# Two row halves of the systolic array taken out of step: one does first products while the other does second products

## The chip, the cores and the metric

The kernel runs on one core of a Trainium2 chip. The metric is the device time of one execution in microseconds (us); lower is better. Three timed executions of the kernel before took 2473.54, 2473.85 and 2474.29 us, median 2473.85 us.

## The reference, cut to what matters

Four sequences of 4096 rows with 192 channels go through a causal convolution over seven positions, with softmax weights by head, and then through two MLPs without bias, 192 to 2048 to 192. Everything is float32.

```python
out = np.einsum('hk,bskhg->bshg', w, x_unf)      # seven taps, 8 heads
x = out.reshape(B * S, D)                        # 16384 x 192
h = x @ w_in1;  x = (h * np.cos(h)) @ w_out1     # first MLP
h = x @ w_in2                                    # second MLP, ELU
out = np.where(h > 0.0, h, np.exp(np.minimum(h, 0.0)) - 1.0) @ w_out2
```

The weights of both MLPs arrive as 64-bit floats (two 32-bit words each) and are decoded on the core.

## The kernel before, in words

**Tiles.** The 16384 tokens are cut into 32 blocks of 512. A block's 192 channels lie on the partitions, as 128 own ones ("o") and 64 more. Every float32 operand is split into a rounded part and a rest (names ending in h and l: xh and xl, gh and gl, wi "h" and "l"), and a product is made of two or three products of parts. All these matmuls contract over 64 rows, so two of them lie side by side on the two row halves of the array (`half`, partitions 0 to 63 and 64 to 127), each with 512 columns of tokens, each into a PSUM bank of its own.

**Steps.** The 2048 hidden columns of an MLP are cut into 16 tiles of 128. A step (m, b, j) is MLP m, block b, and the two hidden tiles 2j and 2j+1. There are 2 x 32 x 8 = 512 steps. The first products of step s (`emit_A`, line 497) are nine matmuls for each of the two tiles: three for the own channels "o", three for the 64 more "c", three for the other half's channels "s" (their copies sh and sl are made by a DMA that swaps the halves). Both tiles advance together, one on each row half, into the banks u and v. The second products of step s - 2 (`emit_B`, line 553; LAG is 2) follow: ten matmuls for each row half, for both tiles, into four accumulators: a0 and a1 belong to row half 0, b0 and b1 to row half 1; a0 and b0 sum the first 128 output channels, a1 and b1 the last 64.

**Between the two products.** A tile u goes through ScalarE and VectorE. First MLP: `emit_act1` (ScalarE, rounds), `emit_mid` (VectorE, subtracts), `emit_act2` (ScalarE, Sin), `emit_g` (VectorE, multiplies with u). Second MLP: `emit_act1` (Relu of -u), `emit_act2` (Exp), `emit_g` (VectorE, the ELU). Then `emit_hi` rounds to gh on ScalarE and `emit_lo` subtracts to gl on GpSimd. `emit_g` is the last reader of the bank. In step s the queues get the gh and gl of step s - 1, and then the two tiles of step s.

**Blocks and groups.** GROUP is 4: the steps run four blocks through the first MLP (a phase of 32 steps), then the same four through the second, eight groups in all. At the end of a block `evac` (line 567) copies a0 and a1 to SBUF on ScalarE and adds b0 and b1 to them on VectorE; `sums` (line 580) then adds the halves, makes zh, zl and zc for the second MLP, or transposes and writes the output. `chore` hands out such work, one piece at a time, between the steps' own instructions.

**Convolution.** The generator `convs` computes the blocks to come, one VectorE instruction (a tap) at a time, each call of `next(cq)` in the second MLP's phases giving one. The first four blocks are done at the start from rows that are transposed on TensorE: `conv_by_products` makes the taps as matmuls for c0, c1, a1, a2 and a3 ("a" is the first 128 channels, "c" the last 64); a0 and c2 go on VectorE.

**Weights.** `pieces` lists 26 pieces of the first MLP's weights and 24 of the second's. `advance` moves three pieces on by one stage each: it decodes one (`decode`, line 163: three or four VectorE instructions, one or two on ScalarE, one on GpSimd), and splits another into its h and l parts. In the first eight steps `advance` is called three times a step, later once, until `prepared`. `need` calls it until the pieces that a step reads are done. The second MLP's pieces start once blocks 0 to 3 are convolved.

**PSUM.** There are eight banks: four accumulators, two for u, one for v (`ps_h`), and one that serves the decoding (`ps_w`) and becomes a second one for v from step 8 on (`top.close()` in `step`; only every other step uses it).

**Order.** The program fixes the order itself (`tc.manual_schedule()`): every engine runs its instructions in the order in which the code names them, and TensorE's queue holds both row halves' matmuls in one order.

## Time and profile before

| | |
|---|---|
| median of three timed executions | 2473.85 us (2473.54 to 2474.29) |
| the profiled execution's own time | 2472.95 us |
| its span, first to last instruction | 2471.2 us |
| mean granted TensorE clock over the span | 0.987 of 2.4 GHz |
| TensorE, matmuls | busy 2349.8 us, 95% |
| VectorE (DVE) | busy 1696.9 us, 69% |
| ScalarE (ACT) | busy 1926.3 us, 78% |
| GpSimd (POOL) | busy 1587.4 us, 64% |

Records of matmuls overlap: one takes 0.39 us in the trace, and two run at a time, one on each row half. In the rows below PE is TensorE, PEld its weight loads, DVE VectorE, ACT ScalarE, POOL GpSimd; "a<-b" is output and input by the program's names, with buffer numbers left out (u, v: the banks of first products; a, b: accumulators of row half 0 and 1; w: a tile between the products; y<-xT,wch: a tap; e: an evacuated sum), and L565 is line 565.

### The profile page before, as it was taken

To read this page: it belongs to the slowest core of one execution; us is meant where nothing else is said; L and a number is where in the kernel's file an instruction comes from. 1 tells how busy PE (TensorE), PEld (TensorE's weight loads), DVE (VectorE), ACT (ScalarE), POOL (GpSimd) and SP (SyncE) were. 2 spreads that over 40 slices of the span, in tenths; PEclk is the share of its full clock that TensorE was granted. 3 is DMA by queue.
4 is the path that set the end of the run, shared out by engine and by line. 5 is a ranking of instruction groups with operands and counts; after the bars stand their busy time and mean duration, and the time that the engine had idled before them with its cause. 6 is when DMAs were issued, how large, how long until landed. Compare 5 with 4: busy or idle time off the path is not lost.

```text
span 2471.2 us, 51323 instructions
## 1 busy us (share of the span) xinstructions
PE 2349.8 (95%) x19614; PEld 1955.0 (79%) x19614; DVE 1696.9 (69%) x2324; ACT 1926.3 (78%) x3529; POOL 1587.4 (64%) x1271
## 2 busy tenths in 40 slices
PE   7888999999999999999999999999999999999998
PEld 4565678777798878987788777987789787888898
DVE  5688895767766586766866678666777668666433
ACT  5566768887788877888788787888778887888886
POOL 4567655666666666666666676666666666667665
PEclk8899999999999999999999999999999999999999
DMA  5012322111221131211221213121222112112011
GB/s 143 26 52 60 71 48 59 42 35 30 60 50 31 27 60 36 54 35 41 45 57 29 48 30 60 37 50 27 38 57 54 31 38 44 41 32 52 19 37 24
DMA packets 279494, 111.89 MB, mean 45 GB/s; under 512 B 231888, under 2 KB 246224, under 8 KB 279248
## 3 DMA queue, kind: packets, MB, share of 16 engines
q1 hardware_dynamic: 278928, 108.35, 20.4%
q8 instruction: 153, 2.51, 0.4%
q14 instruction: 93, 0.76, 0.1%
q10 hardware_dynamic: 320, 0.26, 0.0%
HBM read 29.91 MB, written 12.58 MB: 17 GB/s over the span
## 4 chain that ended last, share of the span: by engine, by line
PE 67%; DVE 12%; ACT 8%; issue 6%; POOL 5%; DMA 0%; SPq 0%; DVEq 0%; POOLq 0%; ACTq 0%
PE a L565 27%; PE u L506 24%; PE v L506 8%; PE b L565 8%; POOL gl L550 4%; ACT gh L545 2%; DVE y L360 2%; DVE e L576 2%; ACT e L584 2%; DVE w L539 2%; DVE w L523 1%; DVE w L185 1%; ACT e L573 1%; DVE w L537 1%; ACT w L516 1%
## 5 line engine op out<-in xcount | busy, mean ns | idle before, releaser
L550 POOL TENSOR_TENSOR gl<-w,gh 128x512 fp32r<-128x512 f32 x1024 | 1348.8, 1322 | 825.6 <-ACT gh L545 741.4
L545 ACT ACTIVATE gh<-w 128x512 fp32r<-128x512 f32 x1024 | 640.3, 625 | 173.6 <-DVE w L537 106.6
L565 PE MATMUL a<-gh,wo_hl 64*128 64x512 f32 x2048 | 638.7, 391 | 2.2 <-ACT gh L545 2.2
L565 PE MATMUL b<-gh,wo_hl 64*128 64x512 f32 x2048 | 636.4, 391 | 0.9 <-DVE e L576 0.9
L565 PE MATMUL a<-gl,wo_hl 64*128 64x512 f32 x1024 | 408.7, 399 | 46.5 <-POOL gl L550 45.2
L565 PEld LDWEIGHTS a<-gh,wo_hl 64*128 64x128 f32 x2048 | 374.3, 185 | 59.9 <-ACT gh L545 19.6
L565 PE MATMUL b<-gl,wo_hl 64*128 64x512 f32 x1024 | 407.7, 398 | 0.0
L506 PE MATMUL u<-sh,wi_o 64*128 64x512 f32 x1024 | 399.8, 390 | 3.7 <-DMA sh<-xh 3.7
L506 PE MATMUL v<-ch,wi_c 64*128 64x512 f32 x1024 | 400.7, 391 | 0.0
L506 PE MATMUL u<-ch,wi_c 64*128 64x512 f32 x1024 | 400.0, 391 | 0.0
L506 PE MATMUL v<-sh,wi_o 64*128 64x512 f32 x1024 | 399.7, 390 | 0.0
L565 PE MATMUL b<-gh,wo_s 64*128 64x512 f32 x1024 | 397.2, 388 | 0.0
L565 PE MATMUL a<-gh,wo_s 64*128 64x512 f32 x1024 | 396.9, 388 | 0.0
L565 PE MATMUL a<-gl,wo_s 64*128 64x512 f32 x1024 | 396.5, 387 | 0.0
L565 PE MATMUL b<-gl,wo_s 64*128 64x512 f32 x1024 | 395.9, 387 | 0.0
L565 PEld LDWEIGHTS b<-gh,wo_hl 64*128 64x128 f32 x2048 | 373.5, 185 | 18.8 <-DVE e L576 3.0
L360 DVE SCALAR_TENSOR_TENSOR y<-xT,wch,y 128x512 f32<-128x512 f32 x264 | 382.1, 1447 | 0.9
L523 DVE SCALAR_TENSOR_TENSOR w<-u,w 128x512 f32<-128x512 f32 x256 | 177.0, 691 | 248.8 <-ACT w L514 247.1
L531 ACT ACTIVATE w<-w 128x512 f32<-128x512 f32 x512 | 323.7, 632 | 16.1
L539 DVE SCALAR_TENSOR_TENSOR w<-w,u 128x512 f32<-128x512 f32 x256 | 174.5, 682 | 193.5 <-ACT w L531 190.5
L529 ACT ACTIVATE w<-w 128x512 f32<-128x512 f32 x512 | 294.7, 629 | 1.6 <-DVE w L523 1.5
L565 PEld LDWEIGHTS a<-gl,wo_hl 64*128 64x128 f32 x1024 | 189.0, 185 | 111.9 <-POOL gl L550 93.0
(129 smaller groups left out, 6930.0 us busy)
## 6 DMA issues: line engine op xcount, KB each, us to landing
out_dram<-e SPq DMA_DIRECT2D x192, 64.0 KB, 1.9
xa<-in_x_dram SPq DMA_DIRECT2D x112, 88.0 KB, 2.6
sh<-xh SPq DMA_DIRECT2D x64, 128.0 KB, 2.3
sl<-xl SPq DMA_DIRECT2D x64, 128.0 KB, 2.3
sh<-zh SPq DMA_DIRECT2D x64, 128.0 KB, 2.4
sl<-zl SPq DMA_DIRECT2D x64, 128.0 KB, 2.3
ch<-zc SPq DMA_DIRECT2D x64, 128.0 KB, 2.3
cl<-zc SPq DMA_DIRECT2D x64, 128.0 KB, 2.3
```

The costliest lines, as they stand in the source:

```text
L185: nc.vector.tensor_scalar(out=bits, in0=size.bitcast(I32), scalar1=3, scalar2=0, op0=ALU.logical_shift_left, op1=ALU.bitwise_or)
L360: nc.vector.scalar_tensor_tensor(out=o, in0=i, scalar=w, in1=o, op0=ALU.mult, op1=ALU.add)
L506: nc.tensor.matmul(u[i], lhsT=at, rhs=x[k + h][p], start=n == 0, stop=n == len(ops) - 1)
L523: nc.vector.scalar_tensor_tensor(out=w, in0=u, scalar=0.25, in1=w.bitcast(I32), op0=ALU.add, op1=ALU.subtract)
L529: nc.scalar.activation(out=w, in_=w, func=AF.Sin, scale=6.283185)
L531: nc.scalar.activation(out=w, in_=w, func=AF.Exp, scale=-1.0)
L539: nc.vector.scalar_tensor_tensor(out=w, in0=w, scalar=-1.0, in1=u, op0=ALU.add, op1=ALU.max)
L545: nc.scalar.activation(out=gh, in_=wrk[s], func=AF.Copy)
L550: nc.gpsimd.tensor_tensor(out=gl, in0=wrk.pop(s), in1=f32(gs[s][0]), op=ALU.subtract)
L565: nc.tensor.matmul(a[o + i], lhsT=w[p, f, :], rhs=g[p], start=first, stop=final)
L576: nc.vector.scalar_tensor_tensor(out=e[i], in0=a[i + 1], scalar=scale, in1=e[i], op0=ALU.mult, op1=ALU.add)
L584: nc.scalar.activation(out=e[3][lo], in_=e[2][hi], func=AF.Copy)
```

## The change: what it does

- **Order on TensorE.** `products` replaces `emit_A` and `emit_B`. In a step, row half 0 does its nine first products (tile 2s, the "even" tile) and then its ten second products; row half 1 does its ten second products and then its nine first products (tile 2s+1, the "odd" tile). `side_by_side` puts them in pairs, 19 a step as before. The first products' parts come in the order c, o, s.
- **Banks.** The tiles take turns in a ring of three banks u0 to u2; once all weights are prepared, the decoding's bank joins as a fourth.
- **Queues.** In `step` the two tiles of a step are handled one after the other: `emit_act1` of tile t, `emit_mid`, then gh and gl of tile t - 1, then `emit_act2` and `emit_g` of tile t.
- **Evacuation.** `evac` copies row half 1's two sums (b0 and b1) on ScalarE, and adds row half 0's (a0, a1) on VectorE, each add in a place of its own.
- **gl.** In the second MLP the gl of odd tiles moves from GpSimd to VectorE, once the weights are prepared.
- **Groups** of 2, 2, 4, 4, ... blocks, nine in all. Only two blocks are prepared from rows at the start; blocks 2 and 3 are convolved on VectorE in the first group's second MLP. The second MLP's weights are wanted from step 16 on, not 32; `advance` is called 1 + s % 2 times a step from step 8 on. In the first list of pieces "o" 1 stands twice now.
- **Start.** Block 0's swapped halves sh and sl come from a matmul with a permutation (`turned`), not from a DMA. Block 1's convolution is put behind the first products of steps 0 and 1.
- **Doubles** for the second MLP are ordered three steps ahead (`AHEAD2`), not six. The buffers of z and of the convolved blocks are laid out anew.

```diff
-GROUP = 4
+GROUPS = (2, 2, 4, 4, 4, 4, 4, 4, 4)
 LAG = 2
 PAIR = 4
 AWAKE = 14
 WARM = 8
-EARLY = 5
 CALLS = 3
-RAW1, RAW2 = 10, 3
+RAW1, RAW2 = 10, 5
 W = 256
-ROWS = 4
-AHEAD = 6
-YA = 3
+ROWS = 2
+AHEAD, AHEAD2 = 6, 3
...
-    ps_h = ctx.enter_context(tc.tile_pool(name="ps_h", bufs=2, space=bass.MemoryType.PSUM))
+    ps_u = ctx.enter_context(tc.tile_pool(name="ps_u", bufs=1, space=bass.MemoryType.PSUM))
     ps_a = ctx.enter_context(tc.tile_pool(name="ps_a", bufs=1, space=bass.MemoryType.PSUM))
-    zt = ctx.enter_context(tc.tile_pool(name="zt", bufs=GROUP))
+    zt = ctx.enter_context(tc.tile_pool(name="zt", bufs=1))
...
+    def turned(y):
+
+        o = ps_a.tile([P, N], F32, tag="a0", name="turned")
+        nc.tensor.matmul(o, lhsT=turn_rows, rhs=y, start=True, stop=True)
+        return o
...
+        yt = turned(ya) if b == 0 else None
         nc.scalar.activation(out=xh, in_=ya, func=AF.Copy)
-        swap(sh, xh)
+        if b == 0:
+            nc.scalar.activation(out=sh, in_=yt, func=AF.Copy)
+        else:
+            swap(sh, xh)
...
-    steps = []
-    for b0 in range(0, NBLK, GROUP):
+    steps, b0 = [], 0
+    for size in GROUPS:
         for m in (1, 2):
-            steps += [(m, b, j) for b in range(b0, b0 + GROUP) for j in range(NP)]
-
-    acc = {}
-    hid = {}
-    wrk = {}
-
-    def emit_A(s):
+            steps += [(m, b, j) for b in range(b0, b0 + size) for j in range(NP)]
+        b0 += size
...
+    ring = deque((ps_u, f"u{k}") for k in range(3))
+    acc, hid, wrk, gs = {}, {}, {}, {}
+
+    def products_A(t):
+
+        (m, b, j), i = steps[t // 2], t % 2
+        x, p = xs[m, b], half[i]
+        pool, tag = ring[0]
+        ring.rotate(-1)
+        u = hid[t] = pool.tile([P, N], F32, tag=tag, name="u")
+        ops = [(k, w, h) for k in "cos" for w, h in (("l", "h"), ("h", "l"), ("h", "h"))]
+        for n, (k, w, h) in enumerate(ops):
+            at = wi[m, w, "c"][p, j] if k == "c" else wi[m, w, "o"][p, j, i if k == "o" else 1 - i]
+            yield u, at, x[k + h][p], n == 0, n == len(ops) - 1
...
+    def products_B(s, i):
+
         m, b, j = steps[s]
-        x = xs[m, b]
-        spare_bank = banks and s % 2 == 0
-        u = [ps_h.tile([P, N], F32, tag="u0", name="u"), (banks[0] if spare_bank else ps_h).tile([P, N], F32, tag="u1", name="v", bufs=1)]
-        ops = [(k, w, h) for k in "ocs" for w, h in (("l", "h"), ("h", "l"), ("h", "h"))]
-        for n, (k, w, h) in enumerate(ops):
-            for i, p in enumerate(half):
-                at = wi[m, w, "c"][p, j] if k == "c" else wi[m, w, "o"][p, j, i if k == "o" else 1 - i]
-                nc.tensor.matmul(u[i], lhsT=at, rhs=x[k + h][p], start=n == 0, stop=n == len(ops) - 1)
-        hid[2 * s], hid[2 * s + 1] = u
+        if (m, b) not in acc:
+            acc[m, b] = [ps_a.tile([P, N], F32, tag=k, name="acc") for k in ("a0", "b0", "a1", "b1")]
+        o, c, p = acc[m, b][i], acc[m, b][2 + i], half[i]
+        h, l, sel = (wo[m, n] for n in ("h", "l", "s"))
+        for f in (2 * j, 2 * j + 1):
+            gh, gl = gs[f"{s} {f % 2}"]
+            st, sp = f == 0, f == NF - 1
+            for to, w, g, first, final in ((o, l, gh, st, False), (o, h, gh, False, False), (c, sel, gh, st, False), (o, h, gl, False, sp), (c, sel, gl, False, sp)):
+                yield to, w[p, f], g[p], first, final
...
+    def side_by_side(*streams):
+
+        for pr in zip_longest(*streams):
+            for product in pr:
+                if product:
+                    o, lhsT, rhs, first, final = product
+                    nc.tensor.matmul(o, lhsT=lhsT, rhs=rhs, start=first, stop=final)
+
+    def products(s):
+        now, then = 0 <= s < total, 0 <= s - LAG < total
+        if not then:
+            side_by_side(products_A(2 * s), products_A(2 * s + 1))
+        elif not now:
+            side_by_side(products_B(s - LAG, 0), products_B(s - LAG, 1))
+        else:
+            side_by_side(chain(products_A(2 * s), products_B(s - LAG, 0)), chain(products_B(s - LAG, 1), products_A(2 * s + 1)))
...
+    def emit_lo(t):
         gl = wk.tile([P, N], F32R, tag="gl", name="gl", bufs=4)
-        nc.gpsimd.tensor_tensor(out=gl, in0=wrk.pop(s), in1=f32(gs[s][0]), op=ALU.subtract)
-        gs[s].append(gl)
-
-    def emit_B(s):
-        m, b, j = steps[s]
-        h, l, sel = (wo[m, n] for n in ("h", "l", "s"))
-        if j == 0:
-            acc[m, b] = [ps_a.tile([P, N], F32, tag=n, name=n) for n in ACC]
-        a = acc[m, b]
-        for q in (0, 1):
-            f = 2 * j + q
-            gh, gl = gs.pop(2 * s + q)
-            st, sp = f == 0, f == NF - 1
-            for o, w, g, first, final in ((0, l, gh, st, False), (0, h, gh, False, False), (2, sel, gh, st, False), (0, h, gl, False, sp), (2, sel, gl, False, sp)):
-                for i, p in enumerate(half):
-                    nc.tensor.matmul(a[o + i], lhsT=w[p, f, :], rhs=g[p], start=first, stop=final)
+        own = gs[f"{t // 2} {t % 2}"]
+        eng = nc.vector if t % 2 and prepared and steps[t // 2][0] == 2 else nc.gpsimd
+        eng.tensor_tensor(out=gl, in0=wrk.pop(t), in1=f32(own[0]), op=ALU.subtract)
...
-        a = acc.pop((m, b))
+        a0, b0, a1, b1 = acc.pop((m, b))
         e = [op.tile([P, N], F32, tag=f"e{i}", name="e") for i in range(4)]
         scale = TWO_PI if m == 1 else 1.0
-        for i in (0, 2):
-            nc.scalar.activation(out=e[i], in_=a[i], func=AF.Copy, scale=scale)
-        yield
-        for i in (0, 2):
-            nc.vector.scalar_tensor_tensor(out=e[i], in0=a[i + 1], scalar=scale, in1=e[i], op0=ALU.mult, op1=ALU.add)
+        add = lambda o, a: nc.vector.scalar_tensor_tensor(out=o, in0=a, scalar=scale, in1=o, op0=ALU.mult, op1=ALU.add)
+        nc.scalar.activation(out=e[0], in_=b0, func=AF.Copy, scale=scale)
+        nc.scalar.activation(out=e[2], in_=b1, func=AF.Copy, scale=scale)
+        yield
+        add(e[0], a0)
+        yield
+        add(e[2], a1)
         chores.append(sums(m, b, e))
...
-            order[0:3] = [(0, 0, 1), (1, 0, 1), ("c", 0, 1), ("o", 1, 1), ("c", 1, 1)]
+            order[0:2] = [("o", 0, 1), ("c", 0, 1), ("o", 1, 1), ("c", 1, 1)]
...
-    begin_at = {max(s - AHEAD, EARLY): (m, b) for (m, b), s in first.items() if (m, b) != (1, 0)}
+    begin_at = {s - (AHEAD, AHEAD2)[m - 1]: (m, b) for (m, b), s in first.items() if (m, b) not in ((1, 0), (1, 1))}
...
+        calls = 0 if prepared else CALLS if s < NP else 1 + s % 2
         if now:
             m, b, j = steps[s]
-            need(m, j + 1, 0, 1, "c")
-            emit_A(s)
-        if s in begin_at:
-            m, b = begin_at[s]
-            chores.append(begin_split(b) if m == 1 else double_z(b))
+            need(m, j + 1, "o", "c")
...
+        products(s)
+        if 0 <= s - LAG < total and steps[s - LAG][2] == NP - 1:
+            finish = evac(*steps[s - LAG][:2])
+        if s in begin_at:
+            m, b = begin_at[s]
+            chores.append(begin_split(b) if m == 1 else double_z(b))
...
+            t = 2 * s + i
+            if now:
+                emit_act1(t)
+            if i == 1:
+                next(finish, None)
+            if now:
+                emit_mid(t)
+            next(finish, None)
+            if 0 <= t - 1 < 2 * total:
+                emit_hi(t - 1)
+                emit_lo(t - 1)
             if calls > i:
                 advance()
-            if first_mlp and i == 1:
-                for q in now:
-                    emit_act2(q)
-                    emit_g(q)
+            if now:
+                emit_act2(t)
+                emit_g(t)
+                if not first_mlp:
+                    next(cq, None)
...
+        if now and not first_mlp and ROWS <= steps[s][1] < ROWS + 2:
             next(cq, None)
-        if prepared and not later:
+        if prepared and len(ring) == 3:
             brief.close()
-            later.append(ctx.enter_context(tc.tile_pool(name="later", bufs=1)))
-
-    later = []
+            top.close()
+            ring.appendleft((ctx.enter_context(tc.tile_pool(name="ps_s", bufs=1, space=bass.MemoryType.PSUM)), "u3"))
...
+            if s == 0:
+                conv_by_products("c", 1)
+                upper_split(1)
+                tokens("a", 1)
+                advance()
+            if s == 1:
+                conv_by_products("a", 1)
+                for _ in split(1):
+                    pass
+                conved.update((0, 1))
+                advance()
+            if s == NP:
+                next(cq)
```

Where the instructions stand, at three places. On TensorE, the middle of a step of the first MLP (u and v are outputs of first products, a0 to b1 or acc the accumulators; the numbers are buffers). Before, the last first products and the first second products:

```order
L506 MATMUL u_14193<-sl_13810,wi1_o_103 128x512
L506 MATMUL v_14194<-sl_13810,wi1_o_103 128x512
L506 MATMUL u_14193<-sh_13809,wi1_o_103 128x512
L506 MATMUL v_14194<-sh_13809,wi1_o_103 128x512
L565 MATMUL a0_14145<-gh_14169,wo1_hl_105 128x512
L565 MATMUL b0_14146<-gh_14169,wo1_hl_105 128x512
```

The same with the change, from the last pair of one step into the next:

```order
L512 MATMUL acc_14079<-gl_14127,wo1_hl_105 128x512
L512 MATMUL u_14166<-sl_13813,wi1_o_103 128x512
L512 MATMUL acc_14081<-gl_14127,wo1_s_106 128x512
L512 MATMUL u_14166<-sh_13812,wi1_o_103 128x512
L512 MATMUL u_14206<-ch_13814,wi1_c_104 128x512
L512 MATMUL acc_14080<-gh_14135,wo1_hl_105 128x512
L512 MATMUL u_14206<-cl_13815,wi1_c_104 128x512
```

A pair was two products of one kind; it is now a second product on one half and a first product on the other, and at the step's border the halves exchange their kinds.

On VectorE, the change of block in the first MLP (w<-u: the subtraction, L523 before and L540 now, or the multiplication, L537 and L554; e: the adds of the evacuation). Before:

```order
L523 SCALAR_TENSOR_TENSOR w_14101<-u_14057,w_14101 128x512
L523 SCALAR_TENSOR_TENSOR w_14104<-v_14058,w_14104 128x512
L576 SCALAR_TENSOR_TENSOR e_14107<-b0_13641,e_14107 128x512
L576 SCALAR_TENSOR_TENSOR e_14109<-b1_13643,e_14109 128x512
L537 TENSOR_TENSOR w_14101<-u_14057,w_14101 128x512
L537 TENSOR_TENSOR w_14104<-v_14058,w_14104 128x512
```

With the change:

```order
L540 SCALAR_TENSOR_TENSOR w_14552<-u_14512,w_14552 128x512
L554 TENSOR_TENSOR w_14552<-u_14512,w_14552 128x512
L575 SCALAR_TENSOR_TENSOR e_14555<-acc_14079,e_14555 128x512
L540 SCALAR_TENSOR_TENSOR w_14567<-u_14533,w_14567 128x512
L575 SCALAR_TENSOR_TENSOR e_14557<-acc_14081,e_14557 128x512
L554 TENSOR_TENSOR w_14567<-u_14533,w_14567 128x512
```

The adds stood together ahead of both multiplications; now the first stands behind the even tile's multiplication, and the second behind the odd tile's subtraction.

On VectorE, the change of block in the second MLP (w<-w,u: the ELU, L539 before and L556 now; y: a tap; xT: the transposition of a block's input; gl at L567). Before:

```order
L539 SCALAR_TENSOR_TENSOR w_16128<-w_16128,u_16084 128x512
L576 SCALAR_TENSOR_TENSOR e_16132<-b0_15662,e_16132 128x512
L576 SCALAR_TENSOR_TENSOR e_16134<-b1_15664,e_16134 128x512
L358 TENSOR_SCALAR y_16141<-xT_16077,wch_100 128x512
L539 SCALAR_TENSOR_TENSOR w_16147<-w_16147,v_16085 128x512
```

With the change:

```order
L567 TENSOR_TENSOR gl_15059<-w_15000,gh_15057 128x512
L556 SCALAR_TENSOR_TENSOR w_15049<-w_15049,u_15009 128x512
L341 SCALAR_TENSOR_TENSOR y_12877<-xT_12822,wch_100,y_12877 128x512
L575 SCALAR_TENSOR_TENSOR e_15051<-acc_14580,e_15051 128x512
L575 SCALAR_TENSOR_TENSOR e_15053<-acc_14582,e_15053 128x512
L556 SCALAR_TENSOR_TENSOR w_15064<-w_15064,u_15030 128x512
L328 STREAM_TRANSPOSE xT_15074<-xc_11822 128x704
L567 TENSOR_TENSOR gl_15130<-w_15064,gh_15128 128x512
```

An odd tile's gl now stands ahead of each even tile's ELU, and a tap stands ahead of the adds instead of behind them.

## Rows read from the trace of the kernel before

**Rows 1.** The page of the whole execution, its first line.

```profile
span 2471.2 us, 51323 instructions
```

**Rows 2.** Stretches, first products (L506) alone: stretch, length, busy (count), PEclk, DMA, GB/s.

```profile
18.50:262.60 244.10, 97.81 (x576) 65.13 (x576) 0.90 0.23 63
262.60:422.70 160.10, 82.70 (x576) 62.94 (x578) 0.97 0.29 55
...
716.30:859.70 143.40, 71.08 (x576) 56.62 (x577) 1.00 0.15 33
859.70:1007.40 147.70, 75.53 (x576) 59.92 (x578) 1.00 0.27 53
```

**Rows 3.** Timeline, TensorE, second MLP: start, length (us), instruction.

```profile
1192.93 0.39 PE L506 MATMUL u<-zh,wi_o 64*128 64x512 f32 x1
...
1197.23 0.39 PE L506 MATMUL u<-zh,wi_o 64*128 64x512 f32 x1
...
1210.60 0.39 PE L565 MATMUL a<-gh,wo_hl 64*128 64x512 f32 x1
...
1210.61 0.39 PE L506 MATMUL v<-sh,wi_o 64*128 64x512 f32 x1
```

**Rows 4.** Timeline, all engines, a change of block; in brackets the wait before it.

```profile
1197.20 1.09 ACT L573 ACTIVATE e<-a 128x512 f32<-128x512 f32 x2 [0.71 <-PE b L565]
...
1197.83 1.29 DVE L576 SCALAR_TENSOR_TENSOR e<-b,e 128x512 f32<-128x512 f32 x2 [0.56 <-ACT e L573]
...
1199.15 0.63 ACT L584 ACTIVATE e<-e 64x512 f32<-64x512 f32 x1 [0.87 <-DVE e L576]
...
1200.48 0.18 PEld L565 LDWEIGHTS a<-gh,wo_hl 64*128 64x128 f32 x1 [0.34 <-ACT gh L545]
...
1201.90 0.50 PE L565 MATMUL a<-gl,wo_hl 64*128 64x512 f32 x1 [0.46 <-POOL gl L550]
...
1202.29 3.87 DVE L360 SCALAR_TENSOR_TENSOR y<-xT,wch,y 128x512 f32<-128x512 f32 x1
...
1208.66 0.50 PE L506 MATMUL v<-zh,wi_o 64*128 64x512 f32 x1 [1.35 <-DVE w L539]
```

**Rows 5.** Stretch of the first eight steps: length; busy of PE, PEld, DVE, ACT, POOL.

```profile
18.60:117.00 98.40, 75.37 (x349) 45.76 (x349) 58.17 (x124) 52.31 (x118) 53.33 (x62) 0.83 0.23 63
```

**Rows 6.** Timeline, TensorE, waits at two steps following each other, first group.

```profile
162.62 0.49 PE L506 MATMUL u<-xh,wi_o 64*128 64x512 f32 x1 [0.35 <-DVE w L537]
168.57 0.49 PE L506 MATMUL u<-xh,wi_o 64*128 64x512 f32 x1 [0.35 <-DVE w L537]
```

**Rows 7.** Groups by line, VectorE, 117 to 262 us: decoding; busy us, mean ns.

```profile
L185 DVE TENSOR_SCALAR w<-t 128x256 int32<-128x256 int32 x22 | 27.9, 1270 | 0.8
...
L184 DVE TENSOR_SCALAR t<-t 128x256 f32<-128x256 f32 x22 | 15.0, 683 | 0.8
L182 DVE TENSOR_SCALAR t<-raw 128x256 int32<-128x256 int32 x22 | 14.2, 645 | 0.0
L186 DVE SCALAR_TENSOR_TENSOR raw<-raw,t 128x256 int32<-128x256 int32 x22 | 9.1, 414 | 0.0
```

**Rows 8.** Timeline, TensorE, a wait in step 0.

```profile
25.05 0.79 PE L506 MATMUL u<-sh,wi_o 64*128 64x512 f32 x1 [3.68 <-DMA sh<-xh]
```

**Rows 9.** Groups by line, VectorE, ScalarE and GpSimd, 860 to 2314 us.

```profile
L360 DVE SCALAR_TENSOR_TENSOR y<-xT,wch,y 128x512 f32<-128x512 f32 x175 | 262.0, 1497 | 0.0
...
L576 DVE SCALAR_TENSOR_TENSOR e<-b,e 128x512 f32<-128x512 f32 x80 | 51.5, 684 | 19.5 <-ACT e L573 18.9
...
L433 DVE TENSOR_TENSOR cl<-y,ch 128x512 fp32r<-128x512 f32 x10 | 6.8, 683 | 0.0
...
L545 ACT ACTIVATE gh<-w 128x512 fp32r<-128x512 f32 x640 | 400.4, 626 | 76.2 <-DVE w L537 43.3 <-DVE w L539 20.4 <-PE v L506 7.7
...
L550 POOL TENSOR_TENSOR gl<-w,gh 128x512 fp32r<-128x512 f32 x640 | 846.7, 1328 | 504.6 <-ACT gh L545 454.0 <-POOL gl L550 17.7 <-PE b L565 14.9
```

More of the change, by code (lines that the diff above doesn't have):

```diff
@@ L174, in decode @@
         bits = w.bitcast(I32)
-        both = two if m == 1 else stage.tile([P, 2, W], F32, tag="t", name="t", bufs=1)
-        size, low = both[:, 0, 0:n], both[:, 1, 0:n]
+        size, low = two[:, 0, 0:n], two[:, 1, 0:n]
         turn[0] += 1
@@ L332, in from_rows @@
         return xT
-    def y_tile(what, b):
-        if what == "a" and b >= GROUP and b % GROUP == GROUP - 1:
-            return later[0].tile([P, N], F32, tag="y", name="y")
-        return yp.tile([P, N], F32, tag="y" + what, name="y", bufs=YA if what == "a" else 2)
     def conv(what, b):
@@ L409, in conv_by_products, with tokens @@
             nc.tensor.matmul(o, lhsT=w, rhs=xT[0:w.shape[0], k * Q:k * Q + N], start=k == 0, stop=k == len(taps) - 1)
[L410 to L414 removed]
         ys[what, b] = o
     xTs = {}
[L419 to L422 removed]
+    def tokens(what, b):
+        xTs[what, b] = from_rows(what, b)
     pair = {}
@@ L585, in sums @@
         yield
-        eng.tensor_tensor(out=e[2][lo], in0=e[2][lo], in1=e[3][lo], op=ALU.add)
+        (nc.vector if last else nc.gpsimd).tensor_tensor(out=e[2][lo], in0=e[2][lo], in1=e[3][lo], op=ALU.add)
         yield
         if m == 1:
-            zh, zl, zc = (zt.tile([P, N], F32R, tag=n, name=n) for n in ("zh", "zl", "zc"))
+            zh, zl, zc = (zt.tile([P, N], F32R, tag=n, name="z") for n in z_tags(b % ZN))
             nc.scalar.activation(out=zh, in_=e[0], func=AF.Copy)
@@ L648, in advance @@
             next(g)
-            for k in ((0, 1) if kind == "o" else (kind,)):
-                ready[k, m] = at
+            ready[kind, m] = at
         if begun:
@@ L659, in advance @@
             prepared.add(True)
-    ready, prepared, banks = {}, set(), []
+    ready, prepared = {}, set()
     def need(m, at, *kinds):
```

214 lines of the change are left out of this document (77 added, 137 removed).

## Prediction, before the change was run

> **What bounds the kernel now.** I read the page first: one core, span 2471.2 us [rows 1]. TensorE's busy share says little, because matmul records overlap, so I read how long its steps take. A step is 18 first products and 20 second products, in 19 pairs, one matmul of each pair on each row half; there are 512 steps. The stretches by first products [rows 2] hold 576 each, so 32 steps: 244.1 us for the first, 160.1 us for the second, and from then on 143.4 us for a phase of the first MLP and 147.7 us for one of the second (seven of each, alike within a few us). The timeline of TensorE [rows 3] gives a step in which nothing waits: one step's first product starts at 1192.93, the next one's at 1197.23, so 4.30 us, or 0.226 us a pair. Thirty-two such steps are 137.6 us. A steady phase thus loses 5.8 us (first MLP) or 10.1 us (second), four blocks in each; the first two phases lose 129.0 us together, and 18.5 us go by before the first step. With 512 x 4.30 = 2201.6 us and some 10 us at the end this makes the span. TensorE's pair rate is the floor; what can be won is some 270 us, and the change moves no matmul of a steady step off it.
>
> Where a steady phase loses is read from the timeline around a change of block [rows 4]. All four accumulators end together. ScalarE waits 0.71 us for them, copies two (1.09 us), then waits 0.87 us for VectorE's two adds (1.29 us) before its next copy; the gh copies queue behind all that, and TensorE waits 0.34 us for weights behind gh and 0.46 us for gl. In the second MLP a convolution tap on VectorE then takes 3.87 us, the next ELU behind it is late, and v's bank holds TensorE for 1.35 us. That is the kind of stall that makes a block 35.9 or 36.9 us instead of 34.4.
>
> **The change, part by part.** *Pairs out of step.* Row half 0 does first products, then second; row half 1 the reverse. The count is the same, 19 pairs. A mixed pair is in the trace already: after the v stall, an "a" product on one half starts at 1210.60 and a "v" product on the other at 1210.61, at the usual pitch [rows 3]. So the step stays 4.30 us; cost 0.
>
> *The new time limits.* A tile's u is done 9 pairs into a step (even tile) or at its end (odd). Its path is ScalarE, VectorE, ScalarE, VectorE, gh on ScalarE, gl on GpSimd: 0.16 us from the last matmul's issue (0.39 - 0.226 us), then with the nearest rows 0.55, 0.65, 0.63, 0.65, 0.63 and 1.33 us [rows 4, 9], so 4.6 us, 5.0 with the queueing behind the next tile's first ScalarE pass. An odd gl is wanted 8 pairs into the step after next: 4.30 + 8 x 0.226 = 6.1 us after the odd tile's end. Before, it was 8.6. So 1.1 us of slack is left, and in quiet steps nothing is lost. The four banks come round after two steps, as before.
>
> *Change of block, first MLP.* In us from the start of the step: half 1 ends its two sums at pair 10, half 0 at pair 19. ScalarE: even tile's pass 2.20 to 2.75, two copies to 3.85 (no wait, where it waited 0.71), old gh to 4.45, Sin to 5.05. VectorE in the new order: g of the even tile 5.05 to 5.70, first add to 6.35, the odd tile's subtraction to 7.00, second add to 7.65 (0.65 each, [rows 4]: 1.29 for two). Half 0 wants its banks back at 4.30 + 2.04 = 6.34 and 6.79. So the second add is 0.85 us late, and this is the new wait. Four blocks, 3.4 us, and 0.4 us for the activation table's change, an estimate: 137.6 + 3.8 = 141.4 us; now 143.4.
>
> *Change of block, second MLP.* Every odd gl moves from GpSimd to VectorE. Nearest row: the all-SBUF subtraction of L433, 0.68 us where GpSimd was out of the way [rows 9]. VectorE: gl 4.45 to 5.10, g to 5.75, a tap to 6.45, adds to 7.10 and 7.75; wanted at 6.34 and, shifted by that 0.76, at 7.55: 0.95 us lost. Three of four blocks have taps; without a tap 0.3. I add 1.0 us a phase for taps that meet GpSimd elsewhere (the 3.87 us kind; GpSimd has half as much to do): 137.6 + 2.9 + 0.3 + 1.0 = 141.8 us; now 147.7. Per pair of phases 2.0 + 5.9 = 7.9 us, seven times: **-55 us**. Ends: all late adds hidden, 275.2 against 291.1 us, -111 us; nothing gained, 0.
>
> *VectorE against GpSimd.* The trace shows the price of an all-SBUF VectorE instruction beside GpSimd: taps take 1.50 us on average, the adds, which read PSUM, 0.68, and L433 0.68 [rows 9]. In the quiet order a VectorE gl follows its gh, by when GpSimd's even gl (1.33 us in 4.30) is over; so I take 0.7. The Trainium skill ("SBUF — State Buffer", Who interferes with whom) says that a VectorE instruction with two SBUF inputs and a GpSimd one exclude each other for the whole instruction, so that moving gl to VectorE would lengthen both; by that price of 1.5 us for each the sum is that of the second rival. The tap row agrees with the rule.
>
> *The first 64 steps.* Now 18.5 + 244.1 + 160.1 = 422.7 us. The groups of two want the second MLP's weights at step 16, not 32, so 24 pieces are decoded at 1.5 a step. In steps 0 to 7 (98.4 us; VectorE busy for 58.2 [rows 5]) the products of blocks 2 and 3, one convolution on VectorE and the 3.68 us wait for sh [rows 8] fall away; the same 26 pieces stay (o1 comes twice). Between 58 and 98 I take 80. From step 8 before, a single v bank holds the loop at 5.95 us (162.62 to 168.57) [rows 6]; three banks end that, and VectorE is next: a piece takes 1.27 + 0.68 + 0.65 + 0.41 = 3.0 us there [rows 7], so a tile with a piece 4.3 us (0.65 + 3.0 + 0.65), one without 1.6. Two steps hold three and one: 14.5 us, eight steps 58. Then seven steps of the second MLP with a tap for each tile: 3 x 4.4 + 2.15 = 15.35 us per two, 54 in all. Nine steps without pieces at 4.45: 40. Two full blocks at the steady rate: 71, and two with three convolution calls a step: 71 + 2. Sum 18.6 + 80 + 58 + 54 + 40 + 71 + 73 = 394.6: **-28 us**. Ends: 370 (pieces at 1.7 us, the 0.41 us row four times, and 70 for the first eight steps) and 435 (nothing gained, and second weights late by 12).
>
> *The end.* The last odd tile is ready half a step later: +1.3 us.
>
> The sum is made against the profiled execution's own 2472.95 us (the span and 1.75 us around it; the median of the three timed runs is 0.9 higher): 2472.95 - 55 - 28 + 1.3 = **2391 us**.
>
> **The rivals.** *1, cleaner than that.* ScalarE's room (2.15 us a tile against 0.55 + 0.63 + 0.63) and a stall's own shift let the late adds vanish. For it: the adds are late by under 1 us. Against: VectorE's order puts the second add behind two instructions of a later tile. Price: -111 - 50 + 1: 2313.
> *2, slower: VectorE blocked by GpSimd.* Place: phases of the second MLP. If every odd gl and every tap takes 1.45 us, a step holds 1.3 (two g) + 1.45 + 1.5 x 1.45 + 0.16 (adds) = 5.1 us of VectorE, over 4.30: a phase 163 us, 15 more than now, so 2473 + 7 x (15 - 2.0) - 28 = 2536. It decides from about 1.34 us a piece, where a phase costs 153.7 and eats the rest of the gain. For it: the 1.50 of the taps. Against: that mean is from a time when GpSimd had both gl.
> *3, slower: the odd tile's path.* If it takes L instead of 5.0 us, L over 6.1, two steps take L + 2.5 us. At 7.5 us a step is 5.0 and the kernel near 2700. It decides from 6.5. For it: GpSimd's extra work at a block's end; against: that comes once in eight steps.
> *4, the start gains nothing:* 2473 - 55 + 13 = 2431. For it: VectorE is the bound there and the pieces come closer together.
> *5, no effect,* late adds costing what the old stalls cost: 2473.
>
> **How the numbers follow.** Forecast (2345 to 2432) 0.66; rival 1 (2300 to 2345) 0.13; rival 4 in its upper part (2432 to 2468) 0.08; rival 5 0.03; rival 2 0.06; rival 3 0.04. About 0.2%, 5 us, can be told from no change: faster 0.87, same 0.03, slower 0.10. The range 2328 to 2445 holds the forecast and about half of rivals 1 and 4 each, some 0.8.
>
> **What would show it.** Right: steady phases of 141 and 142 us; TensorE's waits at a change of block released by the second add; VectorE's gl near 0.7 us, taps under 1.1; the 64th step done by 395 us. Wrong: quiet steps over 4.30 us (rival 3, or the halves do not overlap), gl and taps at 1.4 us with ELUs late (rival 2), or steps 8 to 22 above 7.7 us (rival 4).

## The result, and the profile after

The changed kernel takes 2413.26 us (median of 4 runs, 2411.42 to 2416.16), the kernel before 2473.72 (2473.54 to 2474.29): a ratio of 0.9756, 95% interval 0.9739 to 0.9773. The profiled execution took 2412.27 us. The forecast was 2391, with a range of 2328 to 2445: the side and the range held, and the gain came out at three quarters of what was forecast (between the two profiled executions, 60.7 of 82 us).

The page's first line answers to [rows 1]; stretches of the changed kernel, cut at first products, answer to [rows 2]. Their counts hold all products, first and second, because one line (L512) now issues both. Columns: stretch, length, TensorE busy (count), granted clock as a share of full, DMA share, GB/s.

```profile
span 2410.6 us, 50284 instructions
```

```profile
29.00:247.50 218.50, 162.37 (x1176) 0.90 0.29 73
247.50:397.40 149.90, 144.62 (x1217) 1.00 0.25 49
...
685.40:829.00 143.60, 141.91 (x1219) 1.00 0.15 33
829.00:970.90 141.90, 139.92 (x1219) 1.00 0.28 55
```

Held against the terms of the forecast, in us (a phase goes from its first first product to that of the next one):

| term | forecast | measured |
|---|---|---|
| first product | 18.6 | 29.05 |
| steps 0 to 7, 8 to 15 | 80, 58 | 74.5, 53.9 |
| seven steps, nine steps | 54, 40 | 48.5, 41.6 |
| two full blocks, two with convolutions | 71, 73 | 72.0, 78.0 |
| 64th step ends | 394.6 | 397.4 |
| first-MLP phases, 7 | 141.4 each | 145.65, then 143.54 to 143.62 |
| second-MLP phases, first 6 | 141.8 each | 142.33, then 141.92 to 141.96 |
| last phase and end | 151.6 (156.2 before, less 5.9, plus 1.3) | 154.0 |

The forecast was summed from differences to the kernel before. Counted in the same way, the miss of 21.3 us is roughly 14 in the first MLP's seven phases (each was to lose 2.0 us; together they gained 0.4), 2 in the first six of the second MLP, 2.5 in the last phase and 3 in the first 64 steps. A quiet step takes 4.31 us, as forecast (4.30).

The timeline of the changed kernel shows a change of block in the first MLP. The step began at 1297.06.

```profile
1302.05 0.69 DVE L554 TENSOR_TENSOR w<-u,w 128x512 f32<-128x512 f32 x1 [1.21 <-ACT w L546]
1302.66 0.68 DVE L575 SCALAR_TENSOR_TENSOR e<-acc,e 128x512 f32<-128x512 f32 x1
...
1303.26 0.68 DVE L540 SCALAR_TENSOR_TENSOR w<-u,w 128x512 f32<-128x512 f32 x1
1303.86 0.68 DVE L575 SCALAR_TENSOR_TENSOR e<-acc,e 128x512 f32<-128x512 f32 x1
...
1304.59 0.49 PE L512 MATMUL acc<-gh,wo_s 64*128 64x512 f32 x1 [0.35 <-DVE e L575]
```

It is the order that the forecast drew: g, first add, the odd tile's subtraction, second add, and TensorE held by the second. The step after it, begun at 1301.36, takes 5.17 us, 0.86 over a quiet one (forecast 0.85). What the forecast left out comes three steps further on (the step begun at 1315.15), where GpSimd makes z between the gl; it stands with the waits of weight loads from 685 to 829 us (a first-MLP phase: us in total, times, longest) and in the timeline:

```profile
PEld acc L512 <- DVE e L575: 3.9, 6, 0.9
PEld acc L512 <- POOL gl L567: 2.6, 8, 0.5
```

```profile
1316.03 2.69 POOL L567 TENSOR_TENSOR gl<-w,gh 128x512 fp32r<-128x512 f32 x2
...
1317.38 0.18 PEld L512 LDWEIGHTS acc<-gl,wo_hl 64*128 64x128 f32 x1 [0.46 <-POOL gl L567]
```

On VectorE the groups by line, 685 to 2256 us, answer to the taps and the subtraction of [rows 9]: a tap takes 0.75 us instead of 1.50, and the new gl 0.75.

```profile
L341 DVE SCALAR_TENSOR_TENSOR y<-xT,wch,y 128x512 f32<-128x512 f32 x179 | 134.2, 750 | 0.0
L567 DVE TENSOR_TENSOR gl<-w,gh 128x512 fp32r<-128x512 f32 x162 | 121.8, 752 | 49.6 <-ACT gh L560 43.6 <-issue 3.0
```

At the start the wait for the sh DMA [rows 8] is gone, but VectorE's timeline has a new one. The split of block 0's upper channels (cl) stands ahead of the second tap and waits for products that TensorE has not done yet:

```profile
9.76 0.68 DVE L339 TENSOR_SCALAR y<-xT,wch 128x512 f32<-128x512 f32 x1 [0.47 <-ACT xT L309]
17.41 0.69 DVE L424 TENSOR_TENSOR cl<-y,ch 128x512 fp32r<-128x512 f32 x1 [6.97 <-ACT ch L423]
```

### The profile page after: what moved, and what is told of

Same layout as the page of the kernel before. It is cut to its first block, busy times and chain, and to the rows that moved or that the text cites. A ratio compares the mean times of both kernels' runs of the same rounds, so it can differ in the third digit from the quotient of the medians.

```text
span 2410.6 us, 50284 instructions
## 1 busy us (share of the span) xinstructions
PE 2314.5 (96%) x19576; PEld 1869.3 (78%) x19576; DVE 1651.6 (69%) x2591; ACT 1952.5 (81%) x3524; POOL 1246.1 (52%) x1023
## 4 chain that ended last, share of the span: by engine, by line
PE 59%; DVE 17%; ACT 17%; issue 4%; POOL 1%; DMA 1%; DVEq 0%; SPq 0%; ACTq 0%; POOLq 0%
PE acc L512 31%; PE u L512 29%; ACT gh L560 5%; DVE w L556 3%; ACT w L546 3%; DVE w L554 3%; DVE gl L567 2%; DVE e L575 2%; DVE w L540 2%; ACT w L531 2%; ACT w L548 2%; DVE y L341 1%; ACT e L576 1%; ACT e L577 1%; ACT w L533 1%
## 5 line engine op out<-in xcount | busy, mean ns | idle before, releaser
L567 POOL TENSOR_TENSOR gl<-w,gh 128x512 fp32r<-128x512 f32 x774 | 1002.5, 1295 | 1110.0 <-ACT gh L560 909.4
L512 PE MATMUL acc<-gh,wo_hl 64*128 64x512 f32 x4096 | 1275.6, 392 | 35.6 <-DVE e L575 18.3
L512 PEld LDWEIGHTS acc<-gh,wo_hl 64*128 64x128 f32 x4096 | 743.5, 185 | 127.0 <-DVE e L575 34.0
L512 PE MATMUL u<-ch,wi_c 64*128 64x512 f32 x2048 | 797.4, 391 | 22.3 <-DVE w L554 9.8
L512 PE MATMUL acc<-gh,wo_s 64*128 64x512 f32 x2048 | 800.8, 392 | 12.7 <-DVE e L575 12.7
L512 PE MATMUL acc<-gl,wo_hl 64*128 64x512 f32 x2048 | 801.7, 392 | 6.0 <-POOL gl L567 2.7
L512 PE MATMUL acc<-gl,wo_s 64*128 64x512 f32 x2048 | 797.5, 390 | 0.0
L512 PE MATMUL u<-sh,wi_o 64*128 64x512 f32 x2048 | 792.9, 388 | 0.0
L554 DVE TENSOR_TENSOR w<-u,w 128x512 f32<-128x512 f32 x512 | 353.8, 691 | 336.6 <-ACT w L546 333.5
L556 DVE SCALAR_TENSOR_TENSOR w<-w,u 128x512 f32<-128x512 f32 x512 | 349.5, 683 | 226.0 <-ACT w L548 225.0
L512 PEld LDWEIGHTS acc<-gh,wo_s 64*128 64x128 f32 x2048 | 377.8, 185 | 72.9 <-DVE e L575 35.6
L512 PEld LDWEIGHTS u<-ch,wi_c 64*128 64x128 f32 x2048 | 378.8, 186 | 71.1 <-DVE w L554 14.9
L512 PEld LDWEIGHTS acc<-gl,wo_hl 64*128 64x128 f32 x2048 | 377.9, 185 | 70.1 <-POOL gl L567 26.6
L512 PE MATMUL u<-z,wi_o 64*128 64x512 f32 x1536 | 432.2, 388 | 0.0
L512 PEld LDWEIGHTS u<-sh,wi_o 64*128 64x128 f32 x2048 | 378.2, 185 | 38.2
L512 PE MATMUL u<-cl,wi_c 64*128 64x512 f32 x1024 | 406.0, 398 | 0.0
L512 PEld LDWEIGHTS acc<-gl,wo_s 64*128 64x128 f32 x2048 | 377.7, 185 | 35.4
L512 PE MATMUL u<-xh,wi_o 64*128 64x512 f32 x1024 | 396.9, 390 | 0.3 <-POOL wi_o L208 0.3
L512 PE MATMUL u<-sl,wi_o 64*128 64x512 f32 x1024 | 396.5, 388 | 0.0
L540 DVE SCALAR_TENSOR_TENSOR w<-u,w 128x512 f32<-128x512 f32 x512 | 349.4, 683 | 50.0 <-ACT w L531 49.6
```

The lines of the kernel that those rows point to most:

```text
L512: nc.tensor.matmul(o, lhsT=lhsT, rhs=rhs, start=first, stop=final)
L540: nc.vector.scalar_tensor_tensor(out=w, in0=u, scalar=0.25, in1=w.bitcast(I32), op0=ALU.add, op1=ALU.subtract)
L554: nc.vector.tensor_tensor(out=w, in0=u, in1=w, op=ALU.mult)
L556: nc.vector.scalar_tensor_tensor(out=w, in0=w, scalar=-1.0, in1=u, op0=ALU.add, op1=ALU.max)
L567: eng.tensor_tensor(out=gl, in0=wrk.pop(t), in1=f32(own[0]), op=ALU.subtract)
```

## The experiments

All are edits of the changed kernel, each timed with the kernel before on the same chip. "Phase" is the usual length of a steady phase.

| run | median us | ratio to before, 95% | first-MLP phase | second-MLP phase | 64th step ends |
|---|---|---|---|---|---|
| changed kernel | 2413.26 | 0.9739 to 0.9773 | 143.55 | 141.95 | 397.4 |
| e1 adds first | 2458.58 | 0.9923 to 0.9953 | 143.35 | 150 | 399.5 |
| e2 gl on GpSimd | 2431.61 | 0.9813 to 0.9846 | 143.5 | 143.7 | 401.1 |
| e3 in phase | 2519.94 | 1.0170 to 1.0201 | 150.7 | 149.6 | 408.1 |
| e4 split later | 2402.92 | 0.9698 to 0.9727 | 143.5 | 142.0 | 388.3 |
| e5 three banks | 2414.66 | 0.9747 to 0.9776 | 143.6 | 142.3 | 398.6 |
| e7 adds, then sums | 2409.75 | 0.9725 to 0.9758 | 142.8 | 141.7 | 399.3 |
| e8 adds before gl | 2401.69 | 0.9694 to 0.9723 | 142.8 | 140.95 | 397.0 |
| e9 adds, gl on VectorE | 2431.29 | 0.9814 to 0.9843 | 145.8 | 141.8 | 399.4 |
| e10 z on VectorE | 2400.96 | 0.9694 to 0.9723 | 144.7 | 140.1 | 389.5 |
| e11 sum too, o1 once | 2403.76 | 0.9702 to 0.9735 | 146.5 | 140.0 | 381.8 |
| e12 best | 2381.07 | 0.9611 to 0.9637 | 142.8 | 140.05 | 382.7 |
| e13 best, spaced | 2426.52 | 0.9794 to 0.9821 | 143.1 to 146.4 | 147.1 | 386.4 |

**The halves in phase again (e3).**

```diff
-side_by_side(chain(products_A(2 * s), products_B(s - LAG, 0)), chain(products_B(s - LAG, 1), products_A(2 * s + 1)))
+side_by_side(chain(products_A(2 * s), products_B(s - LAG, 0)), chain(products_A(2 * s + 1), products_B(s - LAG, 1)))
```

> Both row halves do their first products, then both their second products; banks, groups and gl stay as changed. Theory (out of step matters because one half's sums end at half of the step, so that ScalarE copies them without waiting): ScalarE now waits some 1.5 us for the copies with the next tile's work behind it, all four banks come free late, a block loses 2.5 to 3 us in either MLP: phases near 149 and 150 us, kernel 2510 (2450 to 2560). Rival (banks, gl on VectorE and groups carry the gain, the halves' order does not): phases within 2 us of 143.6 and 142, kernel 2405 to 2440.

It took 2519.94 us, 107 more than the changed kernel. The timeline has the wait that out of step removes: ScalarE's copy waits for the sums' end with the next tile's work behind it, so TensorE waits for gh and then for the adds.

```profile
754.61 0.60 ACT L576 ACTIVATE e<-acc 128x512 f32<-128x512 f32 x1 [1.41 <-PE acc L512]
...
758.20 0.73 PE L512 MATMUL acc<-gh,wo_hl 64*128 64x512 f32 x4 [1.39 <-ACT gh L560]
...
759.31 0.49 PE L512 MATMUL acc<-gh,wo_s 64*128 64x512 f32 x2 [0.37 <-DVE e L575]
```

A block loses 1.8 to 3.8 us (means by its place in the phase) instead of 0.25 to 2.2. So the changed kernel can't do without its title part. What that part is worth by itself is not shown: all else here is ordered for it, the kernel before, in phase with another order, lost less, and no run gave an in-phase order the rest of the change.

**The odd gl back on GpSimd (e2).** `eng = nc.gpsimd` in `emit_lo`.

> The odd tiles' gl of the second MLP goes back from VectorE to GpSimd; the rest of the change stays. In the changed kernel the taps take 0.75 us on average, in the kernel before 1.50. Theory (the taps were long because GpSimd was at work nearly all the time): taps back to 1.3 to 1.5 us, steps with taps at a change of block longer, second-MLP phase from 141.95 to 145 (143.5 to 147.7), first-MLP phase as it is, kernel 2430 (2422 to 2452). Rival (VectorE is the fuller engine and gains from being rid of gl): taps may stretch, but the second-MLP phase stays under 142.5 or falls, kernel 2400 to 2415.

2431.61 us, in the theory's range, but not by its mechanism: 1.75 us or a little more in each later second-MLP phase, nearly all of it in the phase's first block (3.9 us lost instead of 2.2), where TensorE waits for GpSimd's gl, and 8.3 us up to the first full one's end (693.7 us instead of 685.4). The taps did not go back to 1.3 or 1.5 us; they took 0.88 (groups by line, 685 to 2250 us):

```profile
L341 DVE SCALAR_TENSOR_TENSOR y<-xT,wch,y 128x512 f32<-128x512 f32 x180 | 157.6, 876 | 0.0
```

GpSimd was busy for 65% of this run, as in the kernel before (64%). So its busy share alone does not make a tap long; the last section shows what does.

**Three banks throughout (e5).** The branch that adds the fourth bank is never taken.

> The fourth bank for u is never added: three banks from start to end. Theory (a tile's bank is read last by g, some 2.6 us after its last product, and wanted again 4.3 to 4.5 us after it, so that three banks do in quiet steps): quiet steps stay at 4.31 us, only changes of block may lose up to 0.3 us more, kernel 2413 to 2425. Rival (the fourth bank is what makes the out-of-step order hold): quiet steps over 4.4 us, kernel 2450 or more.

2414.66 us, 1.4 above the changed kernel: the fourth bank is worth 0.3 us a second-MLP phase, and no quiet step needs it.

**The adds first (e1).** Both `next(finish)` that issue the adds stand behind `emit_act2` and ahead of `emit_g` of the even tile.

> Both of VectorE's adds at a change of block are issued ahead of the even tile's g instead of behind g and behind the odd tile's subtraction. Theory (it is VectorE's order that makes the second add late): in the changed kernel a regular block of the first MLP has one step of 5.17 us where a quiet one is 4.31, and in the second MLP 5.2; the sums of row half 0 end near 1301.5 in the block around 1297, so the two adds would end near 1302.3 and 1303.0, and the banks are wanted at 1303.4 and 1303.85: the loss falls below 0.2 us. The first MLP's phase goes from 143.55 to 140 us, the second's from 141.95 to 139.3, the kernel to 2365 (2355 to 2380). Rival (the 0.86 us is ScalarE's doing, or the g that now waits 0.95 us longer carries the loss on): the loss only moves to a later step, phases within 1 us of 143.6 and 142, kernel 2405 to 2415.

Neither came true: 2458.58 us. In the first MLP the loss moved by a step (4.31, then 5.20 us). The edit did more than meant: it also put `sums` into the chores half a step sooner, so that a ScalarE copy which waits for the second add stood ahead of the odd tile's first pass (timeline of e1):

```profile
735.64 0.63 ACT L588 ACTIVATE e<-e 64x512 f32<-64x512 f32 x1 [0.71 <-DVE e L575]
...
736.17 0.58 ACT L531 ACTIVATE w<-u 128x512 int32<-128x512 f32 x1
```

The second MLP lost 8 us a phase, at its first three blocks; what held each of those steps was not taken apart.

**The adds first, the sums where they were (e7).**

```diff
         add(e[2], a1)
+        yield
         chores.append(sums(m, b, e))
```

> As the run with the adds first, but the list of chores gets the block's sums where the changed kernel has it, after the odd tile's subtraction. The run with the adds first showed, in a block of the first MLP, that ScalarE's copy for the sums (e to e, 64 rows) had moved ahead of the odd tile's first ScalarE pass and waited 0.71 us there for the second add; the odd tile came 1.3 us later and the loss moved to the next step. Theory (VectorE's order makes the add late, and that copy alone spoilt the run): steps with a change of block in the first MLP at most 4.5 us, first-MLP phase 140.3 (139.5 to 141), second-MLP phase 139.2 (138.3 to 140.3), kernel 2366 (2358 to 2378). Rival (the g of the even tile that waits 0.95 us longer is itself enough to lose what the adds win): phases within 1.5 us of 143.6 and 142 or above, kernel above 2400.

2409.75 us, between the two. Handing out the sums later gives 49 us back, some 43 of them in the second MLP's phases; that the copy alone did it is shown for neither MLP. The weight loads' waits for the adds shrink from 46.4 us (685 to 2256 us, changed kernel, first line) to 3.6. But most of what they cost returns as waits for gl (e7, 685 to 2250 us):

```profile
PEld acc L512 <- DVE e L575: 46.4, 76, 1.7
```

```profile
PEld acc L512 <- POOL gl L567: 37.0, 65, 1.1
PEld acc L512 <- DVE gl L567: 18.0, 41, 0.8
...
PEld acc L512 <- DVE e L575: 3.6, 10, 0.4
```

A regular first-MLP block (the second of a phase) lost 0.86 us in its third step and 0.33 in its sixth; now 0.28 in the fourth and 0.83 in the sixth. In all it loses 1.19 in the changed kernel and 1.16 here. In the second MLP the second and third block of a phase went from 0.9 to about 0.5, but the first from 2.2 to 2.8.

**The adds ahead of gl too (e8).** The three `next(finish)` of the even tile stand ahead of `emit_hi`.

> As the run before it in this list, with the two adds also ahead of the odd tile's gl, which the second MLP does on VectorE. Theory: in the first MLP nothing differs (gl is GpSimd's there), phase within 0.3 us of that run; in the second MLP the adds come some 0.7 us sooner, its phase 0.3 to 1.5 us shorter, kernel 2360. Rival (the gl that waits two adds longer misses its 1.1 us of slack): second-MLP phase longer than there by 1 us or more, kernel 2370 to 2390.

2401.69 us: the first MLP as in e7, the second 0.75 us a phase shorter. In the first MLP the gl that is late stands behind z on GpSimd (timeline of e8; the step began at 741.54):

```profile
738.94 1.29 POOL L597 TENSOR_TENSOR z<-e,z 128x512 fp32r<-128x512 f32 x1
740.19 1.29 POOL L567 TENSOR_TENSOR gl<-w,gh 128x512 fp32r<-128x512 f32 x1
741.56 1.29 POOL L600 TENSOR_TENSOR z<-e,z 64x512 fp32r<-64x512 f32 x1
742.92 2.70 POOL L567 TENSOR_TENSOR gl<-w,gh 128x512 fp32r<-128x512 f32 x2
...
744.26 0.50 PE L512 MATMUL acc<-gl,wo_hl 64*128 64x512 f32 x1 [0.52 <-POOL gl L567]
```

**Work taken off GpSimd in the first MLP (e9, e10).** e9 is e7 with the first MLP's odd gl on VectorE; e10 is e8 with e4's edit (below) and the two subtractions for z on VectorE.

> As the run with adds first and sums as changed, and in the first MLP too the odd tiles' gl on VectorE. In the changed kernel a first-MLP block loses 0.3 us in its sixth step, where TensorE waits for a gl that GpSimd does behind the sums of the block before. Theory (GpSimd is too full there): the 0.3 us vanish, first-MLP phase 1 to 1.5 us shorter than without, VectorE's gl near 0.75 us, kernel 8 us faster than without (2358). Rival (an instruction of VectorE with both inputs in SBUF holds GpSimd up and is held up by it, or the adds behind gl are late again): gl at 1.1 us or more, or waits for the adds again; first-MLP phase longer, kernel 5 to 15 us slower than without.

> Adds ahead of gl, the first split behind the convolution, and in the first MLP the subtractions that make zl and the upper rows of zc on VectorE instead of GpSimd. With the adds early, TensorE waits in a first-MLP block 0.82 us in its sixth step for a gl that stands on GpSimd behind the subtraction for zl. Theory (GpSimd's queue is what holds that gl): the sixth step falls to 4.5 us or less, first-MLP phase from 142.8 to 140.3 (139.5 to 141.3), second-MLP phase as there (141), kernel 2401.7 - 10.3 (the split) - 17 = 2374 (2367 to 2383). Rival (the odd tile's path is late by itself there, or VectorE's longer queue makes it late): the wait stays or becomes one for g or gh, first-MLP phase 142.5 or more, kernel 2389 or more.

Both rivals won in the first MLP: 3 us a phase longer in e9 (against e7), 1.9 in e10 (against e8). In e9 TensorE waits for VectorE's gl and for gh (690 to 836 us), with gl no slower than before (0.76 us):

```profile
PEld acc L512 <- DVE gl L567: 5.4, 15, 0.6
PEld acc L512 <- ACT gh L560: 3.9, 8, 0.6
```

What is put on VectorE there stands ahead of the next tile's subtraction or g. In e10 TensorE still waits for a gl of GpSimd, but with z gone GpSimd itself stands idle until that gl's gh comes (timeline of e10):

```profile
736.43 1.29 POOL L567 TENSOR_TENSOR gl<-w,gh 128x512 fp32r<-128x512 f32 x1 [1.16 <-ACT gh L560]
...
737.77 0.18 PEld L512 LDWEIGHTS acc<-gl,wo_hl 64*128 64x128 f32 x1 [0.60 <-POOL gl L567]
```

So GpSimd's queue is not what holds it there. In e10's second MLP, which makes the z of the group's last block, the phase fell by 0.9 us.

**The start (e4, e11).** e4 moves `upper_split(0)` behind the convolution loop. e11 is e10 with the first MLP's 64-row sum on VectorE and `order.remove(("o", 1, 1))`.

> The split of the first upper channels (ch, cl of block 0) is issued behind block 0's convolution instead of ahead of its taps. Theory (cl stands in VectorE's queue ahead of the taps and waits for the products on TensorE: 6.97 us of VectorE idle, first product at 29.05 us): taps start about 7 us sooner, first product at 22 to 24 us, kernel 5 to 7 us faster than the changed one, 2406. Rival (something else ends last there, the load of the weights or the transposes): first product within 1 us of 29, or the gain is lost by the end of the first eight steps; kernel 2411 to 2414.

First product at 21.71 us, as the theory has it; the kernel is 10.3 us faster, more than the 5 to 7 expected, with some 2 us from the first eight steps. What the first product waits for last, here as in the changed kernel, is a piece of weights (timeline of e4):

```profile
21.71 0.50 PE L512 MATMUL u<-ch,wi_c 64*128 64x512 f32 x2 [1.42 <-POOL wi_c L208]
```

> As the run before it, with the 64-row sum of the first MLP on VectorE too, and the first MLP's piece o1, decoded twice in the changed kernel, decoded once. Theory for the sum: the 0.28 us of the fourth step in a first-MLP block, where TensorE waits for a gl while GpSimd goes from gl to that sum, shrinks a little, phase 0 to 1 us shorter. Theory for the piece (VectorE bounds the start at about 3 us a piece): the first eight steps 2 to 4 us shorter. Kernel 2367 (2362 to 2374). Rival (VectorE is no bound in the first eight steps, DMA or GpSimd is): the first eight steps within 1 us, and the kernel within 3 us of the run before.

The first eight steps fell from 72.65 to 69.43 us, and the next phase by 4.55 more, perhaps because second-MLP weights come sooner (not looked at): a piece less is worth 7.7 us at the 64th step. The sum on VectorE cost 1.8 us a first-MLP phase, against the theory.

**What helped, together (e12), and spaced (e13).** e12: e8, e4, o1 once, z on VectorE only for a group's last block. e13: two more `yield` between the z subtractions.

> What helped, put together: adds ahead of gl, the first split behind the convolution, o1 decoded once, and the subtractions for zl and zc on VectorE only for the last block of a group, whose z is made in the second MLP's phase. In the last two runs that phase was 140.05 instead of 141, while the first MLP's was 144.7 instead of 142.8. Theory (VectorE has no room for z in the first MLP, and GpSimd and the odd tile's gl gain from it in the second): phases 142.8 and 140.1, the 64th step's end near 382, kernel 2401.7 - 10.3 - 7 - 6 = 2378 (2372 to 2386), below both kernels. Rival (the gains at the start do not add): 2388 to 2395.

> As the run before it, with two half steps between the subtraction for zl and the one for zc. Theory (in a first-MLP block GpSimd holds up gl in the sixth step because four gl and two z subtractions, 7.8 us, stand in its queue within 8 us): the sixth step falls from 5.1 to 4.6 us or less, first-MLP phase from 142.8 to 141.2, kernel 2367 (2362 to 2374). Rival (one z subtraction alone is too much, as the odd tile's path has no slack left so soon after a change of block): the sixth step stays above 4.9 us, kernel within 3 us of the run before.

e12 took 2381.07 us, 0.9624 of the kernel before (0.9611 to 0.9637) and 32 us under the changed one. e13 lost 45 us again: in a regular first-MLP block the sixth step fell from 5.17 to 4.61 us, but the seventh rose from 4.31 to 4.73. Most of the 45 us came in the second MLP (147 us a phase instead of 140): the empty turns held up the chores behind, so that TensorE waited for z's copies (waits of matmuls, 660 to 2230 us):

```profile
PE u L512 <- DMA ch<-z: 17.2, 5, 4.5
```

## Why the prediction was right, and where it was wrong

- *Quiet steps, rivals 3 and 5, the title part.* A step stays 4.31 us, so the odd tile's path is not too long in every step; and the kernel gained 60 us, so "no effect" did not hold. Taking the title part out of the changed kernel (e3) costs 107 us.
- *Second MLP, 141.8 a phase:* 141.95, in part by luck. gl on VectorE takes 0.75 us (0.7 was taken), so rival 2's 1.45 did not come; undoing it costs 1.75 us a steady phase. The ELU stalls of [rows 4] are gone. The second to fourth block lose 0.90, 0.89 and 0.25 us (0.95, 0.95 and 0.3 were taken). But the 1.0 us a phase for taps that meet GpSimd elsewhere did not come (taps take 0.75 us), and the first block loses 2.2 where 0.95 was taken. ScalarE loads an activation table there too, for 1.28 us (timeline of the changed kernel); the text had that change in the first MLP only, and no run took it out. The two errors cancel.

```profile
832.84 1.28 ACT L548 ACT_TABLE_LOAD   x1
```

- *First MLP, 141.4 a phase:* measured 143.55, the same as the 143.4 before. This is the step that failed, and a size: "Four blocks, 3.4 us, and 0.4 us for the activation table's change". The second add's lateness was right (0.86 in a regular block), but the first block of a phase loses 1.40 there and the third 1.07, 4.2 in all with the table's change (the 0.4 us taken for it came from no row; the first block's excess is 0.54); and the waits for gl behind z, 1.1 us a phase (about 0.33 in three blocks, 0.16 in the first), with some 0.4 of smaller ones, were not in the sum. The text had GpSimd's extra work only as a point for rival 3.
- *Rival 1,* that the late adds vanish by a better order, came true in part in the second MLP (140.95 us a phase in e8, 140.05 in e12) and is refuted for the first in a way neither side had: with the adds early (e7, e8) a regular block still loses 1.15 us, now through gl, and spacing (e13) brings 1.04. The traces show where that sum comes from. In the first MLP a tile goes from ScalarE to VectorE, back to ScalarE and back to VectorE, and the next tile's subtraction (L540) stands behind its g. Behind a change of block, where both queues hold nothing else, subtractions follow each other every 1.99 us; TensorE hands over a tile every 2.15. That is 0.33 us of room a step. At the change itself the adds and the sums' copies stand in between. From the last subtraction ahead of the first copy to the eighth one after it, the changed kernel (first two lines) takes 18.43 us and e8 (last two) 18.39, while TensorE needs 8 x 2.15 = 17.2:

```profile
727.17 0.69 DVE L540 SCALAR_TENSOR_TENSOR w<-u,w 128x512 f32<-128x512 f32 x1
745.60 0.68 DVE L540 SCALAR_TENSOR_TENSOR w<-u,w 128x512 f32<-128x512 f32 x1
```

```profile
725.11 0.69 DVE L540 SCALAR_TENSOR_TENSOR w<-u,w 128x512 f32<-128x512 f32 x1
743.50 0.68 DVE L540 SCALAR_TENSOR_TENSOR w<-u,w 128x512 f32<-128x512 f32 x1
```

  The difference, 1.2 us, is what the block loses, whichever instruction shows the wait. In that stretch neither engine waits for TensorE in the changed kernel; in e8 only the early adds do, 0.56 us, as the sums are not done yet. In e9, e10 and e11, which put more on VectorE, the eight take 19.42, 19.36 and 19.95 us and the block loses 2.17, 1.94 and 2.54. Where the adds' new place did make the eight shorter, in the third block of a phase (18.18 us in e7, 18.42 in the changed kernel), the block loses 1.25 instead of 1.51. No run made them shorter by more, so that the whole loss would go with them is not shown.
- *The start, 394.6:* 397.4. Three of its terms were 4 to 6 us too long, the last one 5 too short, and the first product came 10.45 us later than was taken. Of that delay 7.3 us were a place in VectorE's queue (e4): the text counted the removed work, and did not ask what the moved split waits for with the taps behind it. The other 3.1 stay in e4, where the first product, now one of the part c, waits for the weights of c; the kernel before began with the part o. Rival 4 did not come. Which of the parts (groups, banks, pieces, `turned`) won the 25 us of the first 64 steps was not tried one by one.

## What to carry to other kernels

When a stall is removed at a change of block, look at the slack of the path that the stall had covered: where the path is as tight as the stall was long, the loss turns up again a step or three later under another name, and only its sum over the block tells. Ahead of moving an instruction, list what its queue holds behind it and when its own input is ready: this decided e1, e4 and e13. Moving work between engines costs time if it lands ahead of the new engine's part of the tightest path, and the room on that path is read from the pitch of its instructions in a row (1.99 us against 2.15 here), not from busy shares.
